# SwiGLU feed-forward, 2048 x 640 x 1536: the first six f chunks of block 0 in two row halves, and the loads reordered for it

## The chip, the cores and the metric

The kernel runs on one core of a Trainium2 chip. The metric is the device time of one execution in microseconds (us), the median over several runs. Engines are named as in the profile: PE is TensorE's matmul, PEld its weight load, DVE is VectorE, ACT is ScalarE, POOL is GpSimd and SP is SyncE, whose queue issues most DMAs here.

## What is computed

All tensors are bf16. For x of 2048 rows and D = 640, and F = 1536:

```python
g = silu(x @ w_gate)      # (2048, 640) @ (640, 1536)
u = x @ w_up              # (2048, 640) @ (640, 1536)
out = (g * u) @ w_down    # (2048, 1536) @ (1536, 640)
```

## The kernel before

**Tiles.** The 2048 rows are worked on in four blocks of 512 (`S_BLK`; `HALF` is 256). D is cut into `KD = 5` slices of 128 and F into `KF = 12` chunks of 128. A slice of D is what one matmul contracts over. PE needs x with D on the partitions, so `xT` holds x transposed. The weights stay in SBUF: `wg_sb`, `wu_sb` (gate and up, per slice of D) and `wd_sb` (down).

**One block.** For each f chunk, `proj` runs five matmuls (one per slice of D) into an accumulator `pg` for the gate and five into `pu` for up, in PSUM. `gate` takes silu of `pg` on ACT and multiplies by `pu` on DVE into `aT`. After the 12 chunks come the down projections: `po_t` (the last 128 columns of the output, transposed) and `po_a` (the first 512). Twelve chunks of 2 x 5 matmuls and the down part make a block. The last four rows of x are kept out of the projections: DVE computes them with dot products (`row_dots`), from transposed weights `wgT` and `wuT`, spread over the blocks 1 to 3.

**How x becomes xT.** Rows 0-255 of block 0 are loaded as they are (`x_sb`) and transposed by PE (`transpose_chunk`), with copies by ACT and DVE. All other rows come by a DMA that transposes on its way through the crossbar (`turn_x`): rows 256-511 first, later 512 rows each.

**The loads.** Almost all are issued by SP, in the order of the program text, and run on the same DMA engines. The order is: x rows 0-127 (rows 128-255 by ACT); the gate weights of the first four f chunks (`EARLY`), one DMA of 128 KB for each slice of D (slice 1 by ACT); the crossbar copy of rows 256-511; the up weights of the first four chunks as two DMAs of 320 KB, two chunks each with all of D; then gate and up weights of chunks 4-7 and 8-11 (`W_CHUNKS`), 640 KB each; `wd_sb`; and the crossbar copies of the next rows and of the weights for the dot products.

**The head.** `head` begins block 0 while the loads still come in. After 18 warm-up matmuls and the transposes it runs the gate of four chunks at a time, slice by slice of D: slice 0 in two pieces of 128 rows, slices 1 to 4 on 256 rows, then all five slices on rows 256-511. Four accumulators `pgs` of 512 rows are open meanwhile (tag `gu`, four buffers). Then, chunk by chunk, the up matmuls run on 512 rows, into the buffers `po_a` and `po_b`, each followed by its `gate`. Chunks 4 to 11 of block 0 and the other blocks run in the ordinary loop, on 512 rows. `keep_order` holds the instructions of PE, ACT, DVE and SP to the order of the program.

Of the kernel before, what the change touches and what calls it, by code (L numbers as in the profile page):

```python
# [10 lines left out]
def _body(  # L11
# [8 lines left out]
    nc = tc.nc  # L20
    P = nc.NUM_PARTITIONS
    f32 = mybir.dt.float32
    bf16 = mybir.dt.bfloat16
    ACT = mybir.ActivationFunctionType
    ALU = mybir.AluOpType
# [7 lines left out]
    KD = D // P  # L33
    KF = F // P
    S_BLK = 512
    NSB = S // S_BLK
    SUB = S_BLK // P
    HALF = S_BLK // 2
# [4 lines left out]
    WT_STEP = 4  # L43
    ROW_J = 0
    EARLY = 4
    W_CHUNKS = [(4, 8), (8, 12)]
    assert D % P == 0 and F % P == 0 and S % S_BLK == 0 and D > DA and SUB == 4

    consts = ctx.enter_context(tc.tile_pool(name="consts", bufs=1))
# [2 lines left out]
    psum = ctx.enter_context(  # L52
        tc.tile_pool(name="psum", bufs=2, space=bass.MemoryType.PSUM)
    )
# [3 lines left out]
    xT = consts.tile([P, KD, S], bf16)  # L58
    wg_sb = consts.tile([P, KD, F], bf16)
    wu_sb = consts.tile([P, KD, F], bf16)  # L60
    wd_sb = consts.tile([P, KF, D], bf16)
    aT = consts.tile([P, KF, S], bf16)
# [12 lines left out]
    wg_v = w_gate.rearrange("(kd p) f -> p kd f", p=P)  # L75
    wu_v = w_up.rearrange("(kd p) f -> p kd f", p=P)
    wd_v = w_down.rearrange("(kf p) d -> p kf d", p=P)

    def wslice(a, b):
        return slice(a * P, b * P)  # L80

    def load_w(eng, dst, src, a, b):
        eng.dma_start(out=dst[:, :, wslice(a, b)], in_=src[:, :, wslice(a, b)])
# [20 lines left out]
    def turn_x(r0, r1):  # L104
        nc.sync.dma_start_transpose(out=xT[:, :, r0:r1], in_=xt_v[r0:r1])

    ones = consts.tile([P, P], bf16)
    silu_first = consts.tile([P, 1], f32)
# [4 lines left out]
    for kd in range(KD):  # L113
        eng = nc.scalar if kd == 1 else nc.sync
        eng.dma_start(
            out=wg_sb[:, kd, wslice(0, EARLY)], in_=wg_v[:, kd, wslice(0, EARLY)]
        )
    turn_x(HALF, S_BLK)
    nc.scalar.activation(silu_first[:], ones[:, 0:1], ACT.Silu)  # L119
    for a in range(0, EARLY, 2):  # L120
        load_w(nc.sync, wu_sb, wu_v, a, a + 2)
    for a, b in W_CHUNKS:
        load_w(nc.sync, wg_sb, wg_v, a, b)
        load_w(nc.sync, wu_sb, wu_v, a, b)
# [4 lines left out]
    def turn_w(dst, src, f0, f1):  # L129
# [7 lines left out]
        out=x_row[:],  # L137
        in_=x2[S - T : S, :].rearrange("t d -> (t d)").partition_broadcast(P),
# [29 lines left out]
    def do_dots(n):  # L168
        for _ in range(n):
            next(dots, None)  # L170
# [3 lines left out]
    def warm(n):  # L174
        for _ in range(n):
            nc.tensor.matmul(  # L176
                pw[:, 0:P], lhsT=ones[:], rhs=ones[:], start=True, stop=True
            )

    def transpose_chunk(c, parts):  # L180
        c_sl = slice(c * P, (c + 1) * P)
        for copy, tag, k0, k1 in parts:
            pt = psum.tile([P, k1 - k0, P], bf16, tag=tag, name="pt")
            for kd in range(k0, k1):
                nc.tensor.transpose(  # L185
                    out=pt[:, kd - k0, :],
                    in_=x_sb[:, c, kd * P : (kd + 1) * P],
                    identity=ident[:],
                )
            copy(out=xT[:, k0:k1, c_sl], in_=pt[:])  # L190

    def proj_step(ps, w_sb, fc, sb, c0, c1, kd):
        nc.tensor.matmul(  # L193
            ps[:, c0:c1],
            lhsT=w_sb[:, kd, fc * P : (fc + 1) * P],
            rhs=xT[:, kd, sb * S_BLK + c0 : sb * S_BLK + c1],
            start=(kd == 0 and c0 in (0, HALF)),
            stop=(kd == KD - 1),
        )

    def proj(ps, w_sb, fc, sb, c0, c1):
        for kd in range(KD):
            proj_step(ps, w_sb, fc, sb, c0, c1, kd)

    def gu_tiles():
        pg = psum.tile([P, S_BLK], f32, tag="gu", name="pg", bufs=4)
        pu = psum.tile([P, S_BLK], f32, tag="gu", name="pu", bufs=4)
        return pg, pu

    def gate(pg, pu, sb, fc, n_s):  # L210

        s0 = sb * S_BLK
        sg = work.tile([P, S_BLK], f32, name="sg")
        nc.scalar.activation(sg[:, 0:n_s], pg[:, 0:n_s], ACT.Silu)  # L214
        nc.vector.tensor_tensor(  # L215
            out=aT[:, fc, s0 : s0 + n_s], in0=sg[:, 0:n_s], in1=pu[:, 0:n_s], op=ALU.mult
        )

    def head():
        dve, act = nc.vector.tensor_copy, nc.scalar.copy  # L220
        split = [(act, "po_a", 0, 2), (dve, "po_b", 2, KD)]
        pgs = [
            psum.tile([P, S_BLK], f32, tag="gu", name="pg", bufs=4)
            for _ in range(EARLY)
        ]
        warm(N_WARM)
        for c in range(HALF // P):
            transpose_chunk(c, split)

        steps = [(0, 0, P), (0, P, HALF)]  # L230
        steps += [(kd, 0, HALF) for kd in range(1, KD)]
        steps += [(kd, HALF, S_BLK) for kd in range(KD)]
        for kd, c0, c1 in steps:
            for fc in range(EARLY):
                proj_step(pgs[fc], wg_sb, fc, 0, c0, c1, kd)

        for fc in range(EARLY):
            pu = psum.tile([P, S_BLK], f32, tag=("po_a", "po_b")[fc % 2], name="pu")
            proj(pu, wu_sb, fc, 0, 0, S_BLK)
            gate(pgs[fc], pu, 0, fc, S_BLK)  # L240
        keep_order(mybir.EngineType.PE)
        keep_order(mybir.EngineType.Activation)

    head()
    for sb in range(NSB):
        n_s = S_BLK if sb < NSB - 1 else S_BLK - T
        for fc in range(KF):
            if sb == 0 and fc < EARLY:
                continue
            pg, pu = gu_tiles()  # L250
            proj(pg, wg_sb, fc, sb, 0, n_s)
            proj(pu, wu_sb, fc, sb, 0, n_s)
            gate(pg, pu, sb, fc, n_s)
            if sb > 0 and fc < KF - 2:
                do_dots(2)


        n_t = (SUB if sb < NSB - 1 else SUB - 1) * P
        po_t = psum.tile([P, n_t], f32, tag="po_b", name="po_t")
        for kf in range(KF):  # L260
            nc.tensor.matmul(  # L261
                po_t[:],
                lhsT=wd_sb[:, kf, DA:D],
                rhs=aT[:, kf, sb * S_BLK : sb * S_BLK + n_t],
                start=(kf == 0),
                stop=(kf == KF - 1),
            )
        ot_t = outp.tile([P, n_t], bf16, name="ot_t")
        ot_q = outp.tile([P, n_t], bf16, name="ot_q")
        nc.scalar.copy(ot_t[:], po_t[:])  # L270
        do_dots(3)
        nc.vector.transpose(out=ot_q[:], in_=ot_t[:])  # L272
        for q in range(P // Q):
            nc.scalar.dma_start(
                out=out2[
                    sb * S_BLK : sb * S_BLK + n_t, DA + q * Q : DA + (q + 1) * Q
                ].rearrange("(i r) c -> r i c", r=Q),
                in_=ot_q[q * Q : (q + 1) * Q, :].rearrange("r (i c) -> r i c", c=Q),
            )

        for j in range(SUB):
            s0 = sb * S_BLK + j * P
            last = sb == NSB - 1 and j == SUB - 1
            cols = [(0, DA, "po_a")]
            if last:
                cuts = (0, 288, 480, 576, D)
                cols = list(zip(cuts, cuts[1:], ("po_a", "po_b", "po_a", "po_b")))
            for c0, c1, tag in cols:
                po = psum.tile([P, c1 - c0], f32, tag=tag, name="po_a")
                for kf in range(KF):  # L290
                    nc.tensor.matmul(  # L291
                        po[:],
                        lhsT=aT[:, kf, s0 : s0 + P],
                        rhs=wd_sb[:, kf, c0:c1],
                        start=(kf == 0),
                        stop=(kf == KF - 1),
                    )
                ot = outp.tile([P, c1 - c0], bf16, name="ot" if c1 <= DA else "ot_b")
                if c1 <= DA:
                    nc.scalar.copy(ot[:], po[:])  # L300
                else:
                    nc.vector.tensor_copy(out=ot[:], in_=po[:])  # L302
                eng = nc.sync if c1 < D else nc.scalar
                if 0 < j and not last:
                    do_dots(3)
                if sb == NSB - 1 and j == ROW_J:
                    row_tail()
                eng.dma_start(out=out2[s0 : s0 + P, c0:c1], in_=ot[:])
        if sb == 0:
            turn_x(2 * S_BLK, 3 * S_BLK)  # L310
            turn_w(wgT, wgt_v, KF - WT_STEP, KF)
            turn_w(wuT, wut_v, 0, KF)
            turn_x(3 * S_BLK, 4 * S_BLK)
# [107 lines left out]
```

## Time and profile before

| | |
|---|---|
| median of 3 runs | 163.26 us (163.17 to 163.41) |
| profiled execution | span 161.8 us from the first to the last instruction; no other time of it is given |
| PE | 159.4 us busy (99%), 808 matmuls |
| DVE | 111.0 us busy (69%) |
| ACT | 42.6 us busy (26%) |
| DMA | 15.86 MB, mean 98 GB/s |
| HBM | 6.88 MB read, 2.62 MB written |

The span begins with the first instruction; all times in the text are from there. A row of the chain or of a timeline has start, length, engine, line of the kernel and what is written from what. A row of a group has busy time and the mean of one in ns, then the idle time of the engine before it and what ended most of that. A row of a DMA issue has the size and the time from issue to landing.

### The profile page before, as it was taken

What the parts mean: (1) busy time and instruction counts of PE and PEld (TensorE: products, weight loads), DVE (VectorE), ACT (ScalarE), POOL (GpSimd) and SP (SyncE); (2) the same over time, 40 slices, a digit from 0 to 9 for tenths busy, and PEclk for the clock granted to TensorE, in tenths of its full rate; (3) what the DMA queues carried; (4) which work ended last, traced back from release to release, by engine and by line L of the source; (5) the groups of instructions that cost most, each with busy time, mean ns of one, the idle gap of its engine ahead of it and who ended that gap; (6) DMA issues with size and microseconds to landing.
All of it is one profiled execution on the core that took longest, in us unless ns stands there. A gap on an engine that the chain in (4) does not pass through costs nothing.

```text
span 161.8 us, 2142 instructions
## 1 busy us (share of the span) xinstructions
PE 159.4 (99%) x808; PEld 77.6 (48%) x808; DVE 111.0 (69%) x250; ACT 42.6 (26%) x74; POOL 0.6 (0%) x6
## 2 busy tenths in 40 slices
PE   8999999999999999999999999999999999999995
PEld 7854444444444444444444444444444444445454
DVE  2034223599569999989919999979964999993001
ACT  5051222112222222211222322221214222222121
POOL 1000000000000000000000000000000000000000
PEclk9999999999999999999999999999999999999999
DMA  6999999934189999003110000000321000000312
GB/s 212 231 351 349 361 248 231 222 75 91 34 192 159 235 236 184 4 0 34 65 65 0 0 4 2 0 0 3 62 67 34 0 0 0 0 0 4 48 41 73
DMA packets 41961, 15.86 MB, mean 98 GB/s; under 512 B 33504, under 2 KB 41824, under 8 KB 41952
## 3 DMA queue, kind: packets, MB, share of 16 engines
q1 hardware_dynamic: 33584, 14.93, 37.0%
q10 hardware_dynamic: 8368, 0.80, 3.5%
q8 instruction: 6, 0.10, 0.3%
q14 instruction: 3, 0.02, 0.1%
HBM read 6.88 MB, written 2.62 MB: 59 GB/s over the span
## 4 chain that ended last, share of the span: by engine, by line
PE 97%; DMA 2%; SPq 0%; DVE 0%; issue 0%
PE pg L193 32%; PE pu L193 32%; PE po_a L291 26%; PE po_t L261 6%; DMA wg_sb<-in_w_gate_dram 2%; SPq L86 0%; DVE ot_b L302 0%
## 5 line engine op out<-in xcount | busy, mean ns | idle before, releaser
L193 PE MATMUL pg<-xT,wg_sb 128*128 128x512 bf16 (+3 forms) x264 | 59.8, 363 | 0.1
L193 PE MATMUL pu<-xT,wu_sb 128*128 128x512 bf16 (+1 forms) x240 | 59.1, 379 | 0.0
L215 DVE TENSOR_TENSOR aT<-sg,pu 128x512 bf16<-128x512 f32 (+1 forms) x48 | 32.7, 682 | 32.3 <-PE pu L193 32.3
L214 ACT ACTIVATE sg<-pg 128x512 f32<-128x512 f32 (+1 forms) x48 | 28.4, 597 | 71.2 <-PE pg L193 67.4
L291 PE MATMUL po_a<-wd_sb,aT 128*128 128x512 bf16 (+4 forms) x228 | 42.8, 348 | 0.0
L147 DVE SCALAR_TENSOR_TENSOR prod<-wgT,x_row 128x640 f32<-128x640 bf16 x48 | 39.4, 821 | 1.5 <-DMA wgT<-in_w_gate_dram 0.4
L147 DVE SCALAR_TENSOR_TENSOR prod<-wuT,x_row 128x640 f32<-128x640 bf16 x48 | 39.4, 821 | 1.0
L193 PEld LDWEIGHTS <-wg_sb 128*128 128x128 bf16 x264 | 25.9, 100 | 26.8 <-DMA wg_sb<-in_w_gate_dram 0.4
L193 PEld LDWEIGHTS <-wu_sb 128*128 128x128 bf16 x240 | 23.4, 98 | 28.1 <-DMA wu_sb<-in_w_up_dram 0.3
L291 PEld LDWEIGHTS <-aT 128*128 128x128 bf16 x228 | 20.8, 98 | 21.7
L300 ACT CAST ot<-po_a 128x512 bf16<-128x512 f32 (+2 forms) x17 | 9.5, 559 | 31.8 <-PE po_a L291 20.2
L261 PE MATMUL po_t<-aT,wd_sb 128*128 128x512 bf16 (+1 forms) x48 | 10.4, 366 | 0.0
L261 PEld LDWEIGHTS <-wd_sb 128*128 128x128 bf16 x48 | 4.7, 98 | 5.1
L302 DVE CAST ot_b<-po_a 128x96 bf16<-128x96 f32 (+1 forms) x2 | 0.5, 240 | 9.7 <-PE po_a L291 9.6
L270 ACT CAST ot_t<-po_t 128x512 bf16<-128x512 f32 (+1 forms) x4 | 2.2, 559 | 11.6 <-PE po_t L261 11.6
L147 DVE DVE_READ_ACCUMULATOR prod<-wgT,x_row 128x1 f32 x48 | 3.9, 82 | 0.0
L147 DVE DVE_READ_ACCUMULATOR prod<-wuT,x_row 128x1 f32 x48 | 3.9, 82 | 0.0
L272 DVE STREAM_TRANSPOSE ot_q<-ot_t 128x512 bf16<-128x512 bf16 (+1 forms) x4 | 2.7, 676 | 1.7 <-ACT ot_t L270 1.7
L190 DVE COPY xT<-pt 128x384 bf16<-128x384 bf16 x2 | 0.7, 358 | 2.9 <-PE pt L185 2.9
L176 PE MATMUL pw<-ones 128*128 128x128 bf16 x18 | 2.1, 313 | 0.4 <-DVE ones L109 0.4
L176 PEld LDWEIGHTS <-ones 128*128 128x128 bf16 x18 | 1.8, 147 | 0.4 <-DVE ones L109 0.4
L119 ACT ACT_TABLE_LOAD x1 | 1.3, 1283 | 1.0 <-issue 1.0
(13 smaller groups left out, 4.7 us busy)
## 6 DMA issues: line engine op xcount, KB each, us to landing
wd_sb<-in_w_down_dram SPq DMA_DIRECT2D x1, 1920.0 KB, 13.0
out_dram<-ot SPq DMA_DIRECT2D x15, 128.0 KB, 1.7
wg_sb<-in_w_gate_dram SPq DMA_DIRECT2D x2, 640.0 KB, 7.9
wu_sb<-in_w_up_dram SPq DMA_DIRECT2D x2, 640.0 KB, 8.6
wu_sb<-in_w_up_dram SPq DMA_DIRECT2D x2, 320.0 KB, 4.7
x_row<-in_x_dram SPq DMA_DIRECT2D x1, 640.0 KB, 5.1
wg_sb<-in_w_gate_dram SPq DMA_DIRECT2D x4, 128.0 KB, 3.4
out_dram<-ot_q ACTq DMA_DIRECT2D x12, 32.0 KB, 1.9
```

The lines of the kernel that those rows point to most:

```text
L119: nc.scalar.activation(silu_first[:], ones[:, 0:1], ACT.Silu)
L147: nc.vector.scalar_tensor_tensor(out=prod[:], in0=wT[:, fc, :], scalar=1.0, in1=x_row[:, t, :], op0=ALU.mult, op1=ALU.mult, accum_out=acc[ ...
L176: nc.tensor.matmul(pw[:, 0:P], lhsT=ones[:], rhs=ones[:], start=True, stop=True)
L190: copy(out=xT[:, k0:k1, c_sl], in_=pt[:])
L193: nc.tensor.matmul(ps[:, c0:c1], lhsT=w_sb[:, kd, fc * P : (fc + 1) * P], rhs=xT[:, kd, sb * S_BLK + c0 : sb * S_BLK + c1], start=(kd == 0 ...
L214: nc.scalar.activation(sg[:, 0:n_s], pg[:, 0:n_s], ACT.Silu)
L215: nc.vector.tensor_tensor(out=aT[:, fc, s0 : s0 + n_s], in0=sg[:, 0:n_s], in1=pu[:, 0:n_s], op=ALU.mult)
L261: nc.tensor.matmul(po_t[:], lhsT=wd_sb[:, kf, DA:D], rhs=aT[:, kf, sb * S_BLK : sb * S_BLK + n_t], start=(kf == 0), stop=(kf == KF - 1),)
L270: nc.scalar.copy(ot_t[:], po_t[:])
L272: nc.vector.transpose(out=ot_q[:], in_=ot_t[:])
L291: nc.tensor.matmul(po[:], lhsT=aT[:, kf, s0 : s0 + P], rhs=wd_sb[:, kf, c0:c1], start=(kf == 0), stop=(kf == KF - 1),)
L300: nc.scalar.copy(ot[:], po[:])
```

## The change

The number of chunks in the head goes from four to six (`HALVED = 6`), and the whole of these six chunks is done in halves of 256 rows.

- Chunks 0 to 3, rows 0-255: gate slice by slice as before, then up slice by slice, for four chunks at a time. Gate and up of one chunk share one PSUM buffer (`pair`, 2 x 256 columns). Then their four `gate` steps.
- Chunks 4 and 5, rows 0-255: gate, up, `gate` step, chunk by chunk, in the buffers `po_a` and `po_b`.
- Chunks 0 to 5, rows 256-511: the same, in the buffers `gu`.
- The ordinary loop starts at chunk 6 of block 0.

The loads follow. Up weights of the first four chunks come as five DMAs, one for each slice of D, right behind the gate slices. Then gate and up weights of chunks 4 and 5, 320 KB each; then the crossbar copy of rows 256-511; then gate and up of chunks 6-8 and 9-11. `proj_step`, `proj` and `gate` now take the accumulator's slice and the first row.

```diff
-    W_CHUNKS = [(4, 8), (8, 12)]
+    HALVED = 6
+    W_CHUNKS = [(6, 9), (9, 12)]
...
+    nc.scalar.activation(silu_first[:], ones[:, 0:1], ACT.Silu)
+    for kd in range(KD):
+        nc.sync.dma_start(
+            out=wu_sb[:, kd, wslice(0, EARLY)], in_=wu_v[:, kd, wslice(0, EARLY)]
+        )
+    load_w(nc.sync, wg_sb, wg_v, EARLY, HALVED)
+    load_w(nc.sync, wu_sb, wu_v, EARLY, HALVED)
     turn_x(HALF, S_BLK)
-    nc.scalar.activation(silu_first[:], ones[:, 0:1], ACT.Silu)
-    for a in range(0, EARLY, 2):
-        load_w(nc.sync, wu_sb, wu_v, a, a + 2)
     for a, b in W_CHUNKS:
         load_w(nc.sync, wg_sb, wg_v, a, b)
         load_w(nc.sync, wu_sb, wu_v, a, b)
...
-        steps = [(0, 0, P), (0, P, HALF)]
-        steps += [(kd, 0, HALF) for kd in range(1, KD)]
-        steps += [(kd, HALF, S_BLK) for kd in range(KD)]
-        for kd, c0, c1 in steps:
+        for c0 in range(0, HALF, P):
             for fc in range(EARLY):
-                proj_step(pgs[fc], wg_sb, fc, 0, c0, c1, kd)
-
+                proj_step(pairs[fc][:, 0, c0 : c0 + P], wg_sb, fc, c0, 0, c0 == 0)
+        for kd in range(1, KD):
+            for fc in range(EARLY):
+                proj_step(pairs[fc][:, 0, :], wg_sb, fc, 0, kd, False)
+        for kd in range(KD):
+            for fc in range(EARLY):
+                proj_step(pairs[fc][:, 1, :], wu_sb, fc, 0, kd, kd == 0)
         for fc in range(EARLY):
-            pu = psum.tile([P, S_BLK], f32, tag=("po_a", "po_b")[fc % 2], name="pu")
-            proj(pu, wu_sb, fc, 0, 0, S_BLK)
-            gate(pgs[fc], pu, 0, fc, S_BLK)
+            gate(pairs[fc][:, 0, :], pairs[fc][:, 1, :], fc, 0)
+
+        halves = [(0, fc) for fc in range(EARLY, HALVED)]
+        halves += [(HALF, fc) for fc in range(HALVED)]
+        for r0, fc in halves:
+            if r0 == 0:
+                tag, bufs = ("po_a", "po_b")[fc % 2], 2
+            else:
+                tag, bufs = "gu", 4
+            pair = psum.tile([P, 2, HALF], f32, tag=tag, name="pgu", bufs=bufs)
+            proj(pair[:, 0, :], wg_sb, fc, r0)
+            proj(pair[:, 1, :], wu_sb, fc, r0)
+            gate(pair[:, 0, :], pair[:, 1, :], fc, r0)
...
-            if sb == 0 and fc < EARLY:
+            if sb == 0 and fc < HALVED:
                 continue
```

More of the change, by code (lines that the diff above doesn't have):

```diff
@@ L190, in transpose_chunk, with proj_step, proj, gate @@
             copy(out=xT[:, k0:k1, c_sl], in_=pt[:])
-    def proj_step(ps, w_sb, fc, sb, c0, c1, kd):
+    def proj_step(ps, w_sb, fc, r0, kd, start):
+        n = ps.shape[-1]
         nc.tensor.matmul(
-            ps[:, c0:c1],
+            ps,
             lhsT=w_sb[:, kd, fc * P : (fc + 1) * P],
-            rhs=xT[:, kd, sb * S_BLK + c0 : sb * S_BLK + c1],
-            start=(kd == 0 and c0 in (0, HALF)),
+            rhs=xT[:, kd, r0 : r0 + n],
+            start=start,
             stop=(kd == KD - 1),
         )
-    def proj(ps, w_sb, fc, sb, c0, c1):
+    def proj(ps, w_sb, fc, r0):
         for kd in range(KD):
[L203 to L212, printed above, removed]
+            proj_step(ps, w_sb, fc, r0, kd, kd == 0)
+    def gate(pg, pu, fc, r0):
+        n = pg.shape[-1]
         sg = work.tile([P, S_BLK], f32, name="sg")
-        nc.scalar.activation(sg[:, 0:n_s], pg[:, 0:n_s], ACT.Silu)
+        nc.scalar.activation(sg[:, 0:n], pg, ACT.Silu)
         nc.vector.tensor_tensor(
-            out=aT[:, fc, s0 : s0 + n_s], in0=sg[:, 0:n_s], in1=pu[:, 0:n_s], op=ALU.mult
+            out=aT[:, fc, r0 : r0 + n], in0=sg[:, 0:n], in1=pu, op=ALU.mult
         )
@@ L221, in head @@
         split = [(act, "po_a", 0, 2), (dve, "po_b", 2, KD)]
-        pgs = [
-            psum.tile([P, S_BLK], f32, tag="gu", name="pg", bufs=4)
+        pairs = [
+            psum.tile([P, 2, HALF], f32, tag="gu", name="pgu", bufs=4)
             for _ in range(EARLY)
@@ L247, in _body @@
         for fc in range(KF):
-            if sb == 0 and fc < EARLY:
+            if sb == 0 and fc < HALVED:
                 continue
[L250 to L253, printed above, removed]
+            pg = psum.tile([P, S_BLK], f32, tag="gu", name="pg", bufs=4)
+            pu = psum.tile([P, S_BLK], f32, tag="gu", name="pu", bufs=4)
+            proj(pg[:, 0:n_s], wg_sb, fc, sb * S_BLK)
+            proj(pu[:, 0:n_s], wu_sb, fc, sb * S_BLK)
+            gate(pg[:, 0:n_s], pu[:, 0:n_s], fc, sb * S_BLK)
             if sb > 0 and fc < KF - 2:
```

## The prediction

> **What bounds the kernel now.** I read the page first, for the engine that fills the span:
>
> ```profile
> span 161.8 us, 2142 instructions
> PE 159.4 (99%) x808; PEld 77.6 (48%) x808; DVE 111.0 (69%) x250; ACT 42.6 (26%) x74; POOL 0.6 (0%) x6
> ```
>
> TensorE (PE) is busy for 99% of the span. So the question is how much of the first 17 us, which is all that the change touches, is not matmul work at full pace. The chain of waits in order of time shows the stages there:
>
> ```profile
> 0.45 3.21 DMA wg_sb<-in_w_gate_dram
> 3.71 5.21 PE pg L193 x44
> 8.92 4.37 PE pu L193 x20
> 13.29 1.08 PE pg L193 x5
> ...
> 30.55 2.59 PE po_t L261 x12
> ```
>
> PE waits for the first gate weights until 3.71, then never leaves the chain. From 13.29 to 30.55 there are 16 groups of five 512-column matmuls, 17.26 us, so 0.2158 us per matmul. Inside the first two stages the group times hide small gaps, so I took the timeline of PE in stretches of 0.1 us; the first number is a start:
>
> ```profile
> 3.71 0.29 PE L193 MATMUL pg<-xT,wg_sb 128*128 128x128 bf16 x1
> 4.54 0.59 PE L193 MATMUL pg<-xT,wg_sb 128*128 128x256 bf16 x2
> 4.75 0.59 PE L193 MATMUL pg<-xT,wg_sb 128*128 128x256 bf16 x3
> 4.96 0.60 PE L193 MATMUL pg<-xT,wg_sb 128*128 128x256 bf16 x4
> ...
> 6.38 0.57 PE L193 MATMUL pg<-xT,wg_sb 128*128 128x256 bf16 x3
> 6.57 0.49 PE L193 MATMUL pg<-xT,wg_sb 128*128 128x256 bf16 x3
> ...
> 8.64 0.27 PE L193 MATMUL pg<-xT,wg_sb 128*128 128x256 bf16 x1
> 8.79 0.39 PE L193 MATMUL pu<-xT,wu_sb 128*128 128x512 bf16 x1
> 9.02 0.59 PE L193 MATMUL pu<-xT,wu_sb 128*128 128x512 bf16 x2
> ...
> 13.12 0.38 PE L193 MATMUL pg<-xT,wg_sb 128*128 128x512 bf16 x1
> ```
>
> Between 6.57 and 8.64 lie 19 steps of 256 columns: 0.109 us each. (Before 4.96 they come 0.21 apart, half that pace; the change keeps these instructions and their order.) Two gaps stand out. 6.38 + 0.109 = 6.49, but the next start is 6.57: 0.08 us, on the crossbar copy of rows 256-511. 8.64 + 0.109 = 8.75, but the first up matmul starts at 8.79 and its successor 0.23 later instead of 0.216: 0.055 us, on the up weights. That is all that PE waits there: 0.135 us. A better order of loads cannot win more.
>
> **The change, matmuls.** Both kernels reach 6.49 with the same work: the 8 matmuls of 128 columns and the 16 of 256 on gate slices 1 to 4, rows 0-255. Before, 20 gate matmuls of 256 follow, then 20 up matmuls of 512, and f chunks 4 and 5 (20 of 512): from 13.12 on these last take 20 x 0.2158 = 4.32, so chunk 6 starts at 17.44. After, everything up to chunk 6 is in halves: 20 + 40 x 2 = 100 matmuls of 256 columns, 100 x 0.1089 = 10.89, so without a wait chunk 6 starts at 6.49 + 10.89 = 17.38. In terms: -0.135 for the gaps, +0.08 for 40 splits at 2 x 0.1089 - 0.2158 = 0.002 each; the sum is **-0.05 us**. Twice as many weight loads for these 40 cost nothing more, since the 20 steps at 0.109 each had a weight load of their own (100 ns, below). Behind chunk 6 PE does the same as before.
>
> ```profile
> L215 DVE TENSOR_TENSOR aT<-sg,pu 128x512 bf16<-128x512 f32 (+1 forms) x48 | 32.7, 682 | 32.3 <-PE pu L193 32.3
> L214 ACT ACTIVATE sg<-pg 128x512 f32<-128x512 f32 (+1 forms) x48 | 28.4, 597 | 71.2 <-PE pg L193 67.4
> ...
> L193 PEld LDWEIGHTS <-wg_sb 128*128 128x128 bf16 x264 | 25.9, 100 | 26.8 <-DMA wg_sb<-in_w_gate_dram 0.4
> ```
>
> The silus and products become 12 on 256 columns instead of 6 on 512. Even at the full 0.60 and 0.68 us each fits into the 1.09 us that PE takes for a half chunk, and the first accumulator to be reused, chunk 0's, is wanted only at 10.85, over 2 us after its last matmul (about 8.35). A chunk's gate and up now share one PSUM buffer, so a silu may have to wait for the up matmuls too; that chain, 0.60 + 0.68, ends 1.3 us after them, still well ahead of a reuse four half chunks on. ACT's one early silu only moves in the text, not among ACT's instructions. I book all this at nothing; were silu and product at twice these durations, PE would wait about 0.3 us for each half chunk.
>
> **The change, loads.** PE now wants, by the 0.109 pace: up slices 0 to 4 at 6.49, 6.93, 7.36, 7.80, 8.24; gate weights of chunks 4-5 at 8.67; up weights of chunks 4-5 at 9.21; the crossbar copy at 6.49 + 40 x 0.109 = 10.85; chunks 6 on at 17.38. SP's issue queue, and the time from issue to landing for single issues:
>
> ```profile
> 0.45 1.84 SPq L115 DMA_DIRECT2D wg_sb<-in_w_gate_dram  x4
> 2.33 1.91 SPq L105 DMA_TRANSPOSE xT<-in_x_dram  x1
> 4.29 1.15 SPq L83 DMA_DIRECT2D wu_sb<-in_w_up_dram  x2
> ...
> 10.11 1.67 SPq L125 DMA_DIRECT2D wd_sb<-in_w_down_dram  x1
> 11.83 11.46 SPq L105 DMA_TRANSPOSE xT<-in_x_dram  x1
> ```
> ```profile
> wg_sb<-in_w_gate_dram SPq DMA_DIRECT2D x1, 128.0 KB, 3.4
> xT<-in_x_dram SPq DMA_TRANSPOSE x1, 4.2
> wu_sb<-in_w_up_dram SPq DMA_DIRECT2D x1, 320.0 KB, 4.5
> wu_sb<-in_w_up_dram SPq DMA_DIRECT2D x1, 320.0 KB, 4.9
> wd_sb<-in_w_down_dram SPq DMA_DIRECT2D x1, 1920.0 KB, 13.0
> xT<-in_x_dram SPq DMA_TRANSPOSE x1, 13.5
> ```
>
> A 128 KB slice takes 0.46 us to issue (1.84 / 4) and lands 3.4 after; the last of the gate slices, issued at about 1.85 (0.45 + 3 x 0.46), landed at 5.25. After, SP issues five up slices from 2.33 on in its place: they land from 5.7 to 7.6 in steps of 0.46, each 0.65 us or more before PE wants it. **No wait there.** Issue then goes on at 4.63 (gate 4-5), 5.20 (up 4-5) and 5.77 (crossbar copy), 0.57 apart (1.15 / 2).
>
> The 320 KB loads are the tight ones. The two in the trace landed at 4.29 + 4.5 = 8.8 and 4.86 + 4.9 = 9.8, so 1.0 apart. Behind slices that end at 7.3 (0.40 each) to 7.6, gate 4-5 lands at 8.3 to 8.6 (wanted 8.67) and up 4-5 at 9.3 to 9.6 (wanted 9.21): late by 0.1 to 0.4. The second estimate goes by bytes; the last column is GB/s:
>
> ```profile
> 0.00:2.00 2.00, 1.61 (x16) 1.61 (x17) 0.17 (x1) 0.98 (x1) 0.63 (x6) 1.00 0.48 135
> 2.00:4.00 2.00, 1.85 (x18) 1.50 (x17) 0.72 (x2) 1.25 (x4) 0.00 (x0) 1.00 0.88 287
> 4.00:6.00 2.00, 2.00 (x19) 1.78 (x18) 0.00 (x0) 0.00 (x0) 0.00 (x0) 1.00 1.06 242
> 6.00:8.00 2.00, 2.00 (x20) 1.71 (x19) 0.00 (x0) 0.00 (x0) 0.00 (x0) 1.00 0.78 217
> 8.00:10.00 2.00, 2.00 (x15) 1.18 (x13) 0.00 (x0) 1.37 (x3) 0.00 (x0) 1.00 1.05 348
> ```
>
> By 4.0 us 0.84 MB are through. x, gate and up slices and both 320 KB loads are 2,240 KB = 2.29 MB, so 1.45 MB remain: at 348 GB/s until 8.2, at 287 until 9.05. A load is reported some time after its bytes by this count: the last gate slice 0.7 us after (0.98 MB are reached at 4.6), the second 320 KB up load 1.2 after (1.97 MB reached at 8.6, landed 9.8). So 8.9 to 10.25. I take **9.45** for up 4-5, the middle of the first estimate, which the second contains: PE waits **0.24 us** (0 to 1.04) before chunk 4's up matmuls.
>
> The Trainium skill's page "DMA: Bandwidth & Descriptors", section Specifications, puts the limit of one core's reads from HBM at about 358 GB/s; by it the 1.45 MB would be through at 8.05 and up 4-5 there at 8.75 with the shorter lag, without any wait. The 2-4 us row, 287 with plain loads alone, speaks against that pace so early; the 8-10 us row comes near it.
>
> The crossbar copy landed at 2.33 + 4.2 = 6.53, 1.28 us after the slice ahead of it. At the same distance it now lands at 9.45 + 1.28 = 10.7, and PE, held up by 0.24, wants it at 11.09: nothing. It is tied to the load ahead of it, and PE needs 1.64 us from that load's use to the copy's, so a late load does not make the copy late by itself. The next load, gate 6-8, has over 6 us until 17.38, so the slow stretch behind a crossbar copy (the 6-8 us row) is covered. wd is wanted at about 30.4 (the po_t row of the chain) and was there at 10.11 + 13.0 = 23.1; the queue carries the same bytes, so everything behind it moves by tenths of a microsecond under a cover of several.
>
> Sum: -0.05 + 0.24 = **+0.19 us**. The page gives the profiled execution no time but its span, 161.8; the median of the runs, 163.26, lies 1.46 above. I take that as unchanged: 161.8 + 0.19 + 1.46 = **163.45 us**. A measurement here can tell about 0.2%, 0.33 us, from no change.
>
> **The rivals.**
> A, the loads are in time (the 348 GB/s pace from 4 us on): no wait, -0.05, 163.2. For it: with the crossbar copy out of the way DMA has no slow stretch like the one at 6-8 us. By the Trainium skill's 358 GB/s (page and section above) it would be this one.
> B, slower: up 4-5 lands after 9.59, where the wait passes 0.38 and the sum 0.33. At 287 GB/s and the longer lag it lands at 10.25: +1.04 - 0.05, 164.25. For it: the second 320 KB load did trail its bytes by 1.2. Against: that was behind the stall after a crossbar copy.
> C, slower: the crossbar copy binds. The later one, issued at 11.83, kept SP for 11.46 us and landed at 25.3, 2.2 after wd. At that distance it lands at 9.45 + 2.2 = 11.65 against 11.09: 0.56 more, 164.0. It decides from 1.64 us behind the load ahead. Against: that copy has twice the rows.
> D, faster by over 0.2%: as PE can regain 0.135 at most, it would have to come from the half pace before 4.96 ending earlier. At full pace the steps from 3.71 to 4.96 would take half of the 1.25 us: 162.6. Nothing in the change shortens it.
>
> **How the numbers follow.** Forecast (wait 0.05 to 0.38; 163.25 to 163.6) 0.37, A 0.18, B 0.25, C 0.10, D 0.10. The forecast and A lie within 0.2%: same 0.55; B and C slower: 0.35; D faster: 0.10. Low is A less 0.1 for the spread of the runs, 163.1; high takes in C and the greater part of B, 164.0. That leaves out D and B's end.
>
> **What would show it.** In the trace after: 256-column gate and up steps 0.109 apart from 4.96 on; no gap before the first up step at 6.49; a gap of some 0.2 us before chunk 4's up matmuls near 9.2, put down to the wu_sb DMA; none at the first step on row 256, near 11; chunk 6 at about 17.6 (17.38 + 0.24). A gap over 0.4 at the first place is B, one at the second C, none at both A. Wrong altogether would be a gap behind 17.4, or gaps at ACT and DVE's accumulators.

## The result, and the profile after

The changed kernel is slower. The first series gave 164.38, 165.07, 165.27, 166.56 and 166.69 us (a sixth run, 512.92, was disturbed and counts in no comparison), a ratio of 1.0131 to the kernel before (95% interval 1.0091 to 1.0172). Again, on another series, it took 164.90 against 163.46, 1.0084 (1.0062 to 1.0106). The forecast was 163.45, within 163.1 to 164.0.

The profiled run is the fastest one, of 164.38. Its page, and its chain of waits up to block 1:

```profile
span 163.0 us, 2240 instructions
PE 160.6 (98%) x848; PEld 82.0 (50%) x848; DVE 111.8 (69%) x256; ACT 43.7 (27%) x80; POOL 0.6 (0%) x6
```
```profile
5.29 4.96 DMA wu_sb<-in_w_up_dram
...
10.30 8.36 PE pgu L199 x75
18.66 1.08 PE pg L199 x5
...
31.61 2.59 PE po_t L275 x12
34.20 5.18 PE po_a L305 x24
39.38 0.01 issue
39.38 5.34 PE po_a L305 x24
44.73 1.08 PE pg L199 x5
```

Where PE alone filled the chain from 3.71 on, a DMA now stands in it: the up weights of chunks 4-5, issued at 5.29, landed at 10.25. Chunk 6 follows at 18.49 by the timeline instead of 17.44. Block 0's down part took 10.53 us (44.73 - 34.20) where it was 10.36:

```profile
33.14 10.36 PE po_a L291 x48
43.50 1.08 PE pg L193 x5
```

1.05 + 0.17 is the whole difference of the two spans, 1.2. The 0.17 is a gap behind 17.4, which the prediction had named as a sign of being wrong altogether. PE's starts, as in the prediction:

```profile
6.42 0.62 PE L199 MATMUL pgu<-xT,wg_sb 128*128 128x256 bf16 x3
6.64 0.63 PE L199 MATMUL pgu<-xT,wg_sb 128*128 128x256 bf16 x4
6.78 0.49 PE L199 MATMUL pgu<-xT,wg_sb 128*128 128x256 bf16 x3
6.89 0.49 PE L199 MATMUL pgu<-xT,wg_sb 128*128 128x256 bf16 x3
...
9.94 0.27 PE L199 MATMUL pgu<-xT,wg_sb 128*128 128x256 bf16 x1
10.30 0.28 PE L199 MATMUL pgu<-xT,wu_sb 128*128 128x256 bf16 x1
...
11.94 0.27 PE L199 MATMUL pgu<-xT,wg_sb 128*128 128x256 bf16 x1
```

Two things are to be seen. The half pace (0.21 us a step) lasts until 6.7 here, not 4.96, so PE is some 0.85 us behind the forecast's schedule when it comes to chunk 4. And it still finds no up weights: it could start at 10.05 and starts at 10.30. That this wait, 0.25, is the forecast's 0.24 is chance: the load came 0.8 us later than forecast, and so did PE. Between 11.83 and 11.94, at the first step on row 256, there is no gap.

### The profile page after: what moved, and what is told of

Its sections match the earlier page's. It is cut to its first block, busy times and chain, and to the rows that moved or that the text cites. A ratio compares the mean times of both kernels' runs of the same rounds, so it can differ in the third digit from the quotient of the medians.

```text
span 163.0 us, 2240 instructions
## 1 busy us (share of the span) xinstructions
PE 160.6 (98%) x848; PEld 82.0 (50%) x848; DVE 111.8 (69%) x256; ACT 43.7 (27%) x80; POOL 0.6 (0%) x6
## 4 chain that ended last, share of the span: by engine, by line
PE 93%; DMA 5%; SPq 1%; issue 0%; ACTq 0%; DVE 0%
PE pu L199 28%; PE pg L199 28%; PE po_a L305 26%; PE po_t L275 6%; PE pgu L199 5%; DMA wu_sb<-in_w_up_dram 3%; DMA wg_sb<-in_w_gate_dram 2%; SPq L121 0%; SPq L84 0%; ACTq L87 0%; DVE ot_b L316 0%
## 5 line engine op out<-in xcount | busy, mean ns | idle before, releaser
L199 PE MATMUL pg<-xT,wg_sb 128*128 128x512 bf16 (+1 forms) x210 | 52.1, 379 | 0.0
L199 PE MATMUL pu<-xT,wu_sb 128*128 128x512 bf16 (+1 forms) x210 | 52.1, 379 | 0.0
L216 DVE TENSOR_TENSOR aT<-sg,pu 128x512 bf16<-128x512 f32 (+1 forms) x42 | 28.7, 682 | 21.2 <-PE pu L199 21.2
L215 ACT ACTIVATE sg<-pg 128x512 f32<-128x512 f32 (+1 forms) x42 | 25.1, 596 | 60.2 <-PE pg L199 57.1
L199 PEld LDWEIGHTS <-wg_sb 128*128 128x128 bf16 x274 | 27.4, 102 | 25.6
L199 PEld LDWEIGHTS <-wu_sb 128*128 128x128 bf16 x270 | 26.3, 98 | 25.7 <-DMA wu_sb<-in_w_up_dram 0.4
L216 DVE TENSOR_TENSOR aT<-sg,pgu 128x256 bf16<-128x256 f32 x12 | 4.8, 419 | 10.5 <-ACT sg L215 10.5
L199 PE MATMUL pgu<-xT,wg_sb 128*128 128x256 bf16 (+1 forms) x64 | 9.5, 301 | 0.0
L199 PE MATMUL pgu<-xT,wu_sb 128*128 128x256 bf16 x60 | 8.0, 273 | 0.1
L215 ACT ACTIVATE sg<-pgu 128x256 f32<-128x256 f32 x12 | 4.4, 384 | 10.7 <-PE pgu L199 10.7
```

Of the source, the lines that this page charges most:

```text
L199: nc.tensor.matmul(ps, lhsT=w_sb[:, kd, fc * P : (fc + 1) * P], rhs=xT[:, kd, r0 : r0 + n], start=start, stop=(kd == KD - 1),)
L215: nc.scalar.activation(sg[:, 0:n], pg, ACT.Silu)
L216: nc.vector.tensor_tensor(out=aT[:, fc, r0 : r0 + n], in0=sg[:, 0:n], in1=pu, op=ALU.mult)
```

## The experiments

Theories were named as they arose: **L**, the first loads are late and PE waits at chunk 4; **K**, a waiting PE loses its clock; **P**, the clock's start varies by chance; **D**, DVE's order makes a later wgT felt; **I** and **W**, below.

**Both kernels again (again_after, again_before).**

> The changed kernel again. Theory L (loads): PE waits for the up weights of chunks 4-5, which land at about 10.25 us instead of 9.21; that alone costs about 1.0 us, so 164.2 to 164.5 in every run. Theory K (clock): the wait of up to 1 us also lets the granted clock fall for one or more stretches of 3.4 us; each costs up to 1.7 us, so the runs spread from 164.3 to 166.7, those above 165.5 with a mean clock of 0.99. Rival P (phase): the clock's start only varies by chance from run to run, whatever the kernel; the kernel before spreads as widely.

> The kernel before again, for its spread and the time at which its clock comes up. L and K: 163.2 to 163.7 in every run, mean clock 1.00, PE's clock up at about 5 us. P: a spread of 2 us like that of the changed kernel, with some runs at a clock of 0.99.

Measured: 164.55 to 165.47, and 163.09 to 164.11 (median 163.43), all at a mean clock of 1.00. Both kernels spread by about 1 us in this series, but the two ranges don't meet, so P does not explain the difference. K's 0.99 did not appear; in the first series the two runs near 166.6 had it. (The two new profiles hold no record of the clock; the times leave no room for a lost stretch of 1.7 us.) PE waits for the same load in the new profile: it landed at 10.64. Gate 4-5, at 9.64, holds PE too, for 0.3 us.

```profile
5.23 5.41 DMA wu_sb<-in_w_up_dram
10.69 8.36 PE pgu L199 x75
```

**The wait taken away (no_wait), and filled (fill).**

```diff
-    load_w(nc.sync, wg_sb, wg_v, EARLY, HALVED)
-    load_w(nc.sync, wu_sb, wu_v, EARLY, HALVED)
     turn_x(HALF, S_BLK)
+    load_w(nc.sync, wg_sb, wg_v, EARLY, HALVED)
+    load_w(nc.sync, wu_sb, wu_v, EARLY, HALVED)
...
+            wfc = fc - EARLY if r0 == 0 else fc
+            proj(pair[:, 0, :], wg_sb, wfc, r0)
+            proj(pair[:, 1, :], wu_sb, wfc, r0)
```

> Left out: on rows 0-255, chunks 4 and 5 use the weights of chunks 0 and 1, which are there by then, so these two chunks' values differ; and the crossbar copy is issued ahead of the loads of chunks 4-5. The matmuls, silus and products are as many as in the changed kernel. L and K: no wait for chunk 4 and none on row 256, so 163.2 (-0.05 on the kernel before), no run above 163.8, no gap of PE between 6.5 and 17.4. P: the spread of the changed kernel stays, up to 166. If the halves themselves cost time (silu, PSUM, weight loads), it stays at 164 or above without a wait for a DMA.

> The changed kernel with five matmuls of 512 columns on ones (1.08 us at full clock) where PE would wait: three ahead of chunk 4's gate, two ahead of its up. They depend on no load and nothing reads them. The up weights of chunk 4 land as before, so PE goes on at about 10.3. L: no gain, 164.3, and the spread stays as it is. K: 164.3 to 164.6 and no run at 0.99 or above 165.3, since PE isn't idle. P: spread up to 166.7 as before.

no_wait took 164.33 (1.0040, 1.0022 to 1.0058): a miss for L. Chunk 6 did start at 17.33, earlier than before the change, though PE waited 0.3 us for an up slice. The loss had moved. This is the chain of no_wait in block 0's down part:

```profile
25.33 8.15 DMA wgT<-in_w_gate_dram
...
33.58 0.84 DVE prod L152 x2
...
36.15 0.64 DVE ot_q L287
...
38.28 0.50 ACTq L289
38.79 0.04 issue
38.83 0.59 ACT ot L315
39.42 0.04 issue
39.46 1.24 PE po_a L306 x5
```

Read upwards it is theory D: PE waits for a po_a buffer, which ACT's copy (`ot`) frees; ACT's copy is queued behind ACT's four stores of ot_q; these wait for DVE's transposition; and that stands in DVE's queue behind three dot products, which wait for wgT. In the page of before wgT landed at 31.6, here at 33.5. Block 1 started at 44.64, 1.41 us later than an undisturbed down part would give (32.87 + 10.36 = 43.23).

fill took 164.83 (1.0087, 1.0066 to 1.0108), at most 165.32. PE waited for gate 4-5 here, which landed at 9.72. Its last two matmuls on ones ran until up 4-5 landed, at 10.72, and chunk 4's up followed at 10.77: the load still sets that moment, and filling PE gains nothing. As the clock fell in none of again_after's runs either, it can't tell K from L.

**DVE's order (no_wait_swap, swap_after, swap_before) and a late wgT before the change (late_wgT).**

```diff
-        do_dots(3)
+        if sb > 0:
+            do_dots(3)
         nc.vector.transpose(out=ot_q[:], in_=ot_t[:])
+        if sb == 0:
+            do_dots(3)
```
```diff
     nc.sync.dma_start(out=wd_sb[:], in_=wd_v)
...
+    spare = consts.tile([P, KD, 4 * P], bf16)
+    nc.sync.dma_start(out=spare[:], in_=wg_v[:, :, wslice(8, 12)])
     turn_x(S_BLK, 2 * S_BLK)
```

> The kernel without the wait for chunk 4 (its weights on rows 0-255 stood in for, as there), and in block 0 DVE transposes ot_q ahead of its first three dot products instead of behind them. Theory D (DVE's order): the loads end later, so wgT does; DVE waits for it with the transposition queued behind, ACT's copies of po_a wait for that, and PE for its buffers: 1.4 us in the run without the swap. D: block 0's down part takes 10.36 us again and the time is 162.8 to 163.2. Theory L alone (only the first loads count): no change from 164.3. Rival P (the clock's start by chance): no change but for its spread.

> The changed kernel with the same swap. D: its wait for chunk 4 (about 1 us until chunk 6) hides most of the wait for wgT, so only 0.1 to 0.3 us is won: 164.6 to 164.8, and block 0's down part takes 10.36 us. If DVE's order were all of the loss: 163.4. L: 164.9 as before.

> The kernel before with the same swap. D: its runs above 163.2 are those in which wgT comes late (0.65 us in one profile), so the median falls to 163.0 to 163.2 and the spread becomes smaller. L and P: 163.4 as before.

> The kernel before with one more load of 640 KB (gate weights of chunks 8-11, into a tile that nothing reads) behind wd, so that the transposed copies and wgT come about 1.9 us later and the head is as before. D: DVE starts its dot products 1.5 to 1.9 us later and block 1 begins as much later, less nothing: 164.8 to 165.2. L: the head is untouched, so 163.4.

no_wait_swap: 163.20 against 163.38 (0.9987, 0.9974 to 1.0001). The same DMAs, another place for one DVE instruction, 0.9 us less by the ratios and 1.1 by the medians. Its chain has PE alone again:

```profile
31.00 2.59 PE po_t L276 x12
33.59 6.26 PE po_a L309 x29
...
39.90 4.05 PE po_a L309 x18
43.95 1.08 PE pg L199 x5
```

late_wgT: 164.64 (1.0079, 1.0052 to 1.0107), a little below the expected 164.8 to 165.2, with the head and its order untouched. Block 1 began at 44.60 instead of 43.34, 1.26 us later. That is D from the other side, but only 0.79 of it lies in the down part (11.15 against 10.36), where PE again waits for ACT's copy:

```profile
PE po_a L293 <- ACT ot L302: 0.6, 1, 0.6
```

The other 0.47 was lost in the head, which the edit did not touch: the crossbar copy landed at 6.97 there instead of 6.53, and PE, with an earlier clock, waited for it. swap_after: 164.69 (1.0085, 1.0070 to 1.0100), 0.2 less than without by the medians and nothing by the ratios (1.0084): with the wait at chunk 4 in place, PE comes so late to the down part that wgT hardly matters. So the two losses overlap: the wait alone costs 1.3 to 1.4 us (swap_after), wgT alone 0.7 by the ratio and 0.9 by the medians (no_wait), both together 1.4 (again_after).

The profiles without the swap agree on how they overlap. The down part is longer than 10.36 by 0.80 us, plus wgT's landing, less the start of the first po_a matmul: 0.80 + 33.48 - 32.87 = 1.41 in no_wait, 0.80 + 33.44 - 33.45 = 0.79 in late_wgT, 0.80 + 33.40 - 34.03 = 0.17 in the changed kernel. Where that is below nothing, as in wide and one_up, it takes 10.36.

swap_before: 163.38, no change; my expectation that the late wgT sets the median of the kernel before was wrong. It costs there only now and then (0.65 us in again_before's profile).

**One half of the change each (loads_only, order_only).** The first is the kernel before with the changed lines of the loads, the second the reverse, with `W_CHUNKS` as before.

> The kernel before with the changed order of loads alone: its matmuls want rows 256-511 right after the gate of rows 0-255, at 6.5 us, and the crossbar copy lands at about 11.6. L: PE waits 5.1 us there, chunk 6 starts at 22.4, 168.2 us. K (the clock falls when PE waits): some 1.7 us more, and the record of the clock has a second rise. D adds nothing, since wgT is in time for so late a block.

> The changed order of the matmuls with the loads of before. L: the up weights come as two loads of whole chunks at 8.8 and 9.8 and are wanted slice by slice from 6.5 on, so PE waits about 3.3 us; up of chunks 4-7 lands at 14.0 and holds chunk 4; chunk 6 starts at 22.2, 168.0 us. K: 1.7 us more.

170.5 and 168.0, one run each, 163.15 before. Each half needs the other: with the loads alone PE waits 5.2 us for rows 256-511, with the order alone 3.4 us for up weights. Both show K; stretches of loads_only, then of order_only, where the last three columns are granted clock, DMA share and GB/s:

```profile
5.80:9.10 3.30, 1.11 (x10) 0.85 (x9) 0.00 (x0) 0.00 (x0) 0.00 (x0) 1.00 0.99 263
9.20:15.90 6.70, 3.82 (x19) 2.71 (x19) 0.00 (x0) 0.00 (x0) 0.00 (x0) 0.50 1.08 270
16.00:20.00 4.00, 3.95 (x20) 1.89 (x20) 1.71 (x3) 2.08 (x4) 0.00 (x0) 1.00 1.10 351
```
```profile
3.51:10.30 6.79, 3.34 (x34) 2.47 (x32) 0.55 (x2) 0.37 (x1) 0.00 (x0) 1.00 0.99 269
10.34:13.70 3.36, 3.36 (x18) 2.39 (x17) 0.27 (x1) 0.68 (x3) 0.00 (x0) 0.50 1.10 349
13.80:20.00 6.20, 6.20 (x59) 5.55 (x57) 3.08 (x9) 2.45 (x7) 0.00 (x0) 1.00 1.08 359
```

After the wait the clock is at half for 6.8 us in the one and 3.4 in the other. loads_only comes out 2.3 us above L, as K has it (3.9 us of matmuls at half cost 1.9) with a copy that landed 0.4 late. order_only meets L's 168.0 in spite of K, since PE would have waited for chunk 4's up weights anyway: they landed at 13.64, and PE, at half clock, took them up at 14.12.

**Fewer chunks in halves (four_swap), larger rows (wide).** `HALVED = 4` without the loads of chunks 4-5 ahead, `W_CHUNKS = [(4, 8), (8, 12)]` and the swap; and `W_CHUNKS = [(6, 12)]`.

> The changed order with four chunks in halves in place of six: no loads of chunks 4-5 ahead of the crossbar copy; gate and up of chunks 4-7 and 8-11 as before; and DVE's swap in block 0. L: the copy lands 1.3 us behind the last up slice (7.9), at 9.2, and is wanted at 8.7 to 8.9: a wait of 0.3 to 0.5, chunk 6 at 17.9, 163.7 to 163.9. D without L: 163.2.

> The changed kernel with gate and up of chunks 6-11 as one load each (rows of 1536 bytes instead of 768). If the small rows are what makes the loads end later, wd lands at 24.0 instead of 24.5 and wgT 0.4 sooner. L: the wait for chunk 4 is as before, so 164.6 to 164.9. If the order (the crossbar copy in the middle) makes them late, nothing moves.

four_swap: 164.29 (1.0060, 1.0036 to 1.0084), 0.4 above what I expected. Its chain names a wait I had not priced:

```profile
3.88 5.02 PE pgu L197 x41
8.92 0.39 ACT sg L213
9.34 0.43 DVE aT L214
9.81 4.53 PE pgu L197 x40
```

With four chunks the first accumulator is wanted again as soon as its up is done, and PE waits for silu and product. wide: 165.05 (1.0133, 1.0075 to 1.0191); wd landed at 24.5, as in the changed kernel, and wgT at 34.0, not sooner than its 33.4: larger rows do not bring the loads forward. One of its four runs, 166.93, had the mean clock of 0.99.

**The up slices in fewer DMAs (two_up, one_up).** `(0, 2), (2, KD)`, and `(0, KD)`, in place of five slices.

> The changed kernel with the up weights of chunks 0-3 in two DMAs (slices 0-1 and 2-4) instead of five. Theory I (issue: 0.49 us for each 128 KB holds the DMA engines to 268 GB/s): issue of the loads behind is 1.3 us sooner, gate and up of chunks 4-5 land 0.5 us or more sooner (up at 9.6 to 9.9), the wait shrinks as much: 164.2 to 164.5. Theory W (the engines' own pace): they land at 10.2 to 10.7 as before and the time stays at 164.7 to 165.0.

> The same in one DMA of 640 KB. PE then waits for all of it, at about 7.5, instead of slice 0 at 6.5, but wants chunk 4 the later for it. I: up of chunks 4-5 lands at 9.5 to 9.8, 164.2 to 164.6. W: at 10.2 to 10.7 as before, 164.7 to 165.2.

Up 4-5 landed at 10.23 and 10.74: W, not I. By 8 us 1.91 MB had moved in the changed kernel, 2.01 and 1.92 in these. But two_up took 164.08 (1.0048, 1.0027 to 1.0069), less than W allows. Its profile, of a run of 164.28, doesn't tell why: its clock came up at 6.5, so that PE came late to chunk 4, but chunk 4's up still began with the landing, at 10.28, and the span is 163.0 as in the changed kernel's. Where the 0.6 us by the ratios come from stays open: the landing may lie sooner in most of its runs than in the changed kernel's. one_up took 165.94 (1.0134, 1.0091 to 1.0177), with 2.1 us of waiting for the whole of the up weights; one run at 0.99 took 168.44.

## Why the prediction was wrong, step by step

**Matmuls, -0.05: right.** no_wait_swap runs all the halves without the waits and is 0.2 us faster than the kernel before (-0.42 to +0.02). Weight loads, silus and accumulators cost nothing with six chunks; with four they would have (four_swap), so that booking holds by the two half chunks in between.

**Up slices and crossbar copy in time: right in the changed kernel's profile.** The slices landed at 5.7 to 7.9, 0.3 later than forecast at the end; the copy 1.30 us behind the load ahead of it (1.28 forecast), 0.4 ahead of need. Where the clock came up early, a slice was too late after all: fill and wide waited 0.3 us for the last one, which landed at 8.3.

**Up weights of chunks 4-5 at 9.45: the term that was mis-sized.** They landed at 10.25 to 11.0 over the profiles with this order of loads, and chunk 6 hangs on them: it starts 8.24 us behind the landing in the changed kernel (18.49 - 10.25), again_after (18.88 - 10.64), swap_after (18.98 - 10.74) and wide (19.23 - 10.99), whether the clock came up at 6.7 us (the changed kernel) or at 3.4 (wide). In place of the sum's 0.24 the wait cost 1.3 to 1.4 us (swap_after). I took the middle of an estimate by landing steps and let go the slow end of the estimate by bytes, 10.25, which came nearer: rival B, with its 1.04 us. Gate 4-5, forecast for 8.3 to 8.6, landed at 9.3 to 10.0, which in swap_after and wide held PE by 1.1 us before the up weights did. Part of the miss is that the steps were taken from one profile: the second up load of the kernel before landed at 9.8 in it, and at 9.9 to 10.3 in four others with the same first loads (again_before, order_only, swap_before, late_wgT). The rows of the changed kernel show the pace, to be held against 287 and 348:

```profile
4.00:6.00 2.00, 2.00 (x15) 1.57 (x14) 0.25 (x1) 0.00 (x0) 0.00 (x0) 1.00 0.91 283
6.00:8.00 2.00, 2.00 (x17) 1.68 (x16) 0.00 (x0) 0.00 (x0) 0.00 (x0) 1.00 0.85 259
8.00:10.00 2.00, 2.00 (x21) 1.74 (x18) 0.20 (x1) 0.62 (x3) 0.00 (x0) 1.00 1.16 251
10.00:12.00 2.00, 1.92 (x18) 1.54 (x17) 1.63 (x5) 1.08 (x4) 0.00 (x0) 1.00 1.02 256
```

From 4 to 8 us, without a crossbar copy among them, the loads did move faster than the mix before (242 and 217); but by 10 us they were no further than it, 2.41 MB against 2.46. The pace of 348 came only after 12 us, at 342. The Trainium skill's page "DMA: Bandwidth & Descriptors" (Specifications) gives about 358 GB/s as the limit of one core's HBM traffic; no row of the changed kernel reaches it before 12 us. Part of why these rows stay at 251 to 283 is in the traces of both kernels: a packet of 1024 bytes took 46 ns in the median, one of 512 bytes (the loads of two chunks) 27, one of 256 bytes (the crossbar copy, here from 9 us on) 18. Sixteen engines without a pause would by this estimate move 356, 303 and 228 GB/s. So 348, seen with packets mostly of 1024 bytes, was out of reach for the loads of chunks 4-5; no run gave these two larger rows. Why the engines pause from 4 to 8 us (busy shares of 0.91 and 0.85) is open; one DMA for the slices did not bring more by 8 us.

**"Everything behind moves by tenths under a cover of several": wrong.** The cover was checked for wd alone. wgT had none. The waits of the kernel before, between 30 and 46 us, already showed DVE waiting for it, and I did not follow what is queued behind that wait on DVE and ACT:

```profile
ACT ot L300 <- DMA out_dram<-ot_q: 3.2, 1, 3.2
...
DVE prod L147 <- DMA wgT<-in_w_gate_dram: 0.4, 1, 0.4
```

By 14 us the bytes were 0.26 MB behind (3.61 against 3.87), and wgT came 1.8 us later than in that page, worth 0.7 to 0.9 us by itself in no_wait. How much of the 1.8 is the change's is open: with the loads of before, wgT landed at 33.1 in again_before and at 32.9 in swap_before, and with the changed ones at 33.2 to 34.0.

**The clock's rise at 4.96, taken as given: wrong.** It lies between 3.4 us (wide) and 6.7 (the changed kernel) in the traces' record of the clock, where the steps go from 0.21 to 0.11 us. (The clock column of the rows reads 1.00 also ahead of the first record.) In the changed kernel a late rise hides part of the wait and an early one lengthens it, so it moves the time little; and a wait can cost a stretch of clock. The runs of 166.6 to 168.4 in the changed kernel, wide and one_up all had a mean of 0.99, which is what one stretch of 3.4 us at half makes of 165 (1.7 / 165 = 1%). That they are such falls is inferred from the mean: no trace of the changed kernel itself shows one. Rival D, a gain by an earlier rise, was not seen: the early rises (3.4 in wide, 3.5 in swap_after) only met a longer wait.

No version here beats the kernel before beyond its interval. By no_wait_swap, taking these waits from the changed order would bring about 0.2 us, 0.4 at most.

## What to carry to other kernels

When loads are reordered, price every consumer of the queue, not only the first: look for any existing wait on a late load, however small, and follow it through the in-order queues behind it. Splitting work in halves of rows doubles the pace at which PE asks for weights; compare the bytes wanted by each time with the slowest pace seen in that stretch, not the middle one. Take the landing of a load from several profiles: one is a single draw, and here it was the earliest. And once a test without the suspected wait leaves much of the loss, look for where the next wait took its place.

## What was unexpected of the hardware

PE's granted clock came up at 3.4 to 6.7 us after the start in profiles of much the same head, and fell again after waits that were shorter than I had thought to matter. In order_only there are 3.0 us between two starts from 5.84 on and another 1.0 us from 8.94, and the clock was at half from 10.3 to 13.7; in the 3.4 us ahead of that PE was busy for 0.8 us. In swap_after, with waits of 1.14 and 0.37 us and PE busy for 2.3 us of the same stretch (6.92 to 10.33), it held:

```profile
9.69 0.72 PE L199 MATMUL pgu<-xT,wg_sb 128*128 128x256 bf16 x5 [1.14 <-DMA wg_sb<-in_w_gate_dram]
10.78 0.28 PE L199 MATMUL pgu<-xT,wu_sb 128*128 128x256 bf16 x1 [0.37 <-DMA wu_sb<-in_w_up_dram]
```

The Trainium skill's page "TensorE: Matmul & The Clock Gate" (HAM oscillation) names idle gaps of over about 3.4 us as the ones that bite; here two gaps, each below that, were enough.
